# Long convolution and gated projection on one core: scratch and matrix tiles three and four deep, and the last two chunks' taps moved into the next batch's third stage

## The chip, the cores and the metric

The kernel runs on one core of one Trainium2 chip. The metric is the device time of one execution in microseconds (us); the number shown for a kernel is the median of several executions. A TensorE (PE) works out matrix products into PSUM, VectorE (DVE), ScalarE (ACT) and GpSimd (POOL) work on tiles, and SyncE (SP) issues the transfers. Each engine takes its own instructions in order.

## The reference

`x` is [8, 6400, 128] (batch, time, channel) and `h` is [6400, 128]. What is computed, cut to its core:

```
y    = irfft(rfft(x, 12800) * rfft(h, 12800))[:, :6400]      # causal convolution along time, per channel
gate = sigmoid(sum over k of conv_w[k] * shift(y, 4 - k))    # 5 taps along time, per channel
out  = (gate * (y @ w_val)) @ w_out                          # two 128x128 projections
```

All is float32.

## The kernel before

The convolution is a two-step Fourier transform written as matrix products. Time is split as 6400 = 100 x 64 (`N1`, `N2`), and the kernel goes through the eight batches one after another. A batch passes four stages, and the stages of neighbouring batches overlap:

- **First stage (`Forward`)**: 16 groups of eight channels. A group is loaded (224 KB), multiplied by `r1` on PE, and copied from PSUM to the big tile `gy` by DVE (even groups) or ACT (odd groups).
- **Second stage (`Product`)**: 13 blocks `kb` of eight frequencies (the last has four). PE multiplies a block of `gy` by a matrix tile of `m2` (512 KB, `m2_sb`, `M2B` buffers, loaded again for every batch) into a pair of PSUM banks. `swap` (ACT, two instructions) writes the real and the imaginary part exchanged into a scratch tile `w_t`; `mul_u` (DVE) multiplies the PSUM pair by one half of the filter's spectrum, `mul_t` (DVE) the scratch by the other, and `add` (POOL, DVE for the last block) puts their sum back into `gy`. The spectrum comes from DRAM, two tiles of 512 KB for each block (`h_load`, buffers for two blocks).
- **Third stage (`s3_quad`)**: 16 groups, each two PSUM banks of four channels. PE multiplies `gy` by `r3`; ACT copies the first bank (A) and DVE the second (B) to the big tile `dt`. In the same group PE does one group of the first stage for the next batch, so that `gy` is filled again.
- **Fourth stage (`Chunk`)**: the 64 rows of `N2` are cut into a head of four rows (60 to 63, worked first) and 12 chunks of five rows. For a chunk PE does 20 (head: 16) small matmuls from `dt` (`s4`) into one PSUM bank `p`; ACT copies `p` to the tile `y`, writes tap 4 scaled into the gate's rows, and tap 3 scaled into a scratch `q` (`copies`); one step later DVE adds taps 0, 1 and 2 from PSUM and POOL adds `q` (`taps`). Then `project` (PE), `sigm` (ACT), `gate` (DVE), `output` (PE) and `store` (ACT copy and transfer) follow, spread over the next steps.

The fourth stage of a batch and the second stage of the next run together in 13 steps `s` (lines 550 to 579). Step `s` holds the product `s + 1`, the `s4` and the `copies` of chunk `s`, the products' DVE work for block `s`, the `taps` of chunk `s - 1`, and `project`, `sigm` and `gate` of chunk `s - 2`, `output` of `s - 3` and `store` of `s - 4`. Step 0 has two products. Chunk 0 is the head. What is left of the last chunks (`finish`, in five pieces, `trail`) runs with the next batch's third stage: one piece before it and one behind each of its first groups. The head is finished last, since its gate rows take taps of the last chunk.

The order on each engine is the program's (`keep_in_program_order`, line 88, through which every instruction passes: so every row of the profile has L88). Semaphores between the engines, and which of the buffers of a PSUM pool a tile gets, are set by the framework when it compiles. PSUM has two pairs of banks for products and first-stage groups (`pair`, `ps2`), and four single banks (`single`, `ps1`) which third-stage banks, `p`, `project` and `output` share.

The gate's rows and `y` of the chunks below row `LATE` lie in columns of `dt` that `s4` has read already; those from `LATE` on have tiles of their own (`gl`, `yl`), because the next third stage writes `dt` while they are still worked on.

The very first part of the program works out the filter's spectrum (`Spectrum`) together with the products of batch 0, with no fourth stage beside it. In the last batch there is no next batch and so no product.

The lines that the change touches most:

```
M2B = 3
LATE = 30
w_t = [cp.tile([128, KB * C], F32, name=f"w_{i}") for i in range(2)]
self.t = kdt(w_t[kb % 2], kb)
```

Of the kernel before, what the change touches and what calls it, by code (L numbers as in the profile page):

```python
# [9 lines left out]
F32 = mybir.dt.float32  # L10
# [5 lines left out]
C = 128  # L16
N1 = 100
# [3 lines left out]
KB = 8  # L21
# [6 lines left out]
CH = 5  # L28
HEAD = (60, 4)
CHUNKS = [HEAD] + [(a, CH) for a in range(0, 60, CH)]  # L30
NCH = len(CHUNKS)
OUT_ORDER = CHUNKS[1:] + [HEAD]
LATE = 30
LATER = 7
M2B = 3
HB = 4
XB = 4

# [62 lines left out]
def longconv_moe(ctx: ExitStack, tc: tile.TileContext, x, h, r1, m2, r3, m4, w64, out):  # L101
# [4 lines left out]
    cp = ctx.enter_context(tc.tile_pool(name="cp", bufs=1))  # L106
# [12 lines left out]
    w_sb = cp.tile([C, NW], F32, name="w_sb")  # L119
    wc_sb = w_sb[:, 2 * C :]  # L120
    gl = cp.tile([128, N2 - LATE, N1], F32, name="gl")
    yl = {a: cp.tile([128, CH, N1], F32, name=f"yl_{a}") for a, _ in CHUNKS if a >= LATE}
    m2_sb = [cp.tile([128, KB, C], F32, name=f"m2_{i}") for i in range(M2B)]
    h_sb = [cp.tile([128, KB * C], F32, name=f"h_{i}") for i in range(HB)]
    x_sb = [cp.tile([PX, XG, N2], F32, name=f"x_{i}") for i in range(XB)]
    w_t = [cp.tile([128, KB * C], F32, name=f"w_{i}") for i in range(2)]
    p_t = [cp.tile([128, CH, N1], F32, name=f"p_{i}") for i in range(2)]
    hd = dp.tile([NKB, 2, 2 * N2, KB * C], F32, name="hd")

# [60 lines left out]
    act = nc.scalar.copy  # L190
# [9 lines left out]
    class Forward:  # L200


        def __init__(self, src, dst):
            self.src, self.dst, self.n, self.i = src, dst, 0, 0
# [31 lines left out]
    def count(kb):  # L236
        return min(KB, N1 - kb * KB)

    def m2_load(kb):
        if kb < NKB:  # L240
            n = count(kb)
            nc.sync.dma_start(m2_sb[kb % M2B][:, :n], m2[:, kb * KB : kb * KB + n])

    def h_load(kb):
        if kb < NKB:
            n = count(kb) * C
            for r in range(2):
                nc.sync.dma_start(h_sb[(2 * kb + r) % HB][:, :n], hd[kb, r, :, :n])
# [6 lines left out]
    def kdt(t, kb):  # L255
        n = count(kb)
        return t[:, : n * C].rearrange("p (d k t) -> p d k t", k=n, t=2)

    def s2_mm(src, kb):
        pt = pair()  # L260
        n = count(kb)
        for k in range(n):
            nc.tensor.matmul(
                pt[:, k // 4, (k % 4) * C : (k % 4 + 1) * C],
                lhsT=m2_sb[kb % M2B][:, k, :],
                rhs=src[:, :, kb * KB + k],
                start=True,
                stop=True,
            )
        if n <= 4:  # L270
            return pt[:, 0, : n * C].rearrange("p (k d t) -> p d k t", t=2, d=C // 2)
        return pt.rearrange("p b (k d t) -> p d (b k) t", t=2, d=C // 2)
# [24 lines left out]
    class Product:  # L297
        def __init__(self, kb, h=None):
            self.kb, self.v = kb, s2_mm(gy, kb)
            self.t = kdt(w_t[kb % 2], kb)  # L300
            self.u = gy[:, :, kb * KB : kb * KB + count(kb)]
            self.h = [kdt(i, kb) for i in h or [h_sb[(2 * kb + r) % HB] for r in range(2)]]

# [14 lines left out]
    def s3_quad(d0):  # L318
        pt = single()
        for q in range(4):  # L320
            d = d0 + q
            nc.tensor.matmul(
                pt[:N1, q * 2 * N2 : (q + 1) * 2 * N2],
                lhsT=gy[:, d // 2, :, d % 2],
                rhs=r3_sb,
                start=True,
                stop=True,
            )
        o = dv[:N1, :, :, d0 : d0 + 4].rearrange("p n c d -> p (n c) d")
        return lambda e: e(o, pt[:N1].rearrange("p (d m) -> p m d", d=4))  # L330
# [6 lines left out]
    def cells(x, n):  # L337

        out, i = [], 0
        while i < n:  # L340
            y = x + i
            end = 4 if y < 4 else LATE if y < LATE else N2
            k = min(n - i, end - y)
            s = (y - 4) % N2
            out.append((i, gl[:, y - LATE : y - LATE + k] if y >= LATE else dv[:, s : s + k, 1, :N1]))
            i += k
        return out

    class Chunk:


        def __init__(self, b, ch):
            self.b, self.ch = b, ch
            a, n = ch
            self.y = yl[a][:, :n] if a >= LATE else dv[:, a : a + n, 0, :N1]

        def s4(self):
# [22 lines left out]
        def copies(self):  # L380
            a, n = self.ch
            if a == HEAD[0]:
                for i, o in cells(0, n):
                    nc.gpsimd.memset(o[:, :, :1], 0.0)
                    self.first(4, o[:, :, 1:], self.p[:, i : i + n, : N1 - 1])
                act(self.y, self.p)
                for i, o in cells(a, n):
                    self.first(0, o, self.p)
                return
            k = min(n, HEAD[0] - a - 4)  # L390
            for i, o in cells(a + 4, k):
                self.first(4, o, self.p[:, i : i + o.shape[1]])
            act(self.y, self.p)
            self.q = p_t[a // CH % 2]
            self.first(3, self.q, self.p)

        def taps(self):
            a, n = self.ch
            if a == HEAD[0]:
                for j in range(1, 4):  # L400
                    for i, o in cells(a + j, n - j):
                        self.more(j, o, self.p[:, : n - j])
                    for i, o in cells(0, j):
                        self.more(j, o[:, :, 1:], self.p[:, n - j :, : N1 - 1])
                return
            k = HEAD[0] - a - 4
            if k < n:
                for i, o in cells(HEAD[0], n - k):
                    self.more(4, o, self.p[:, k:])
            for j in range(3):  # L410
                for i, o in cells(a + j, n):
                    self.more(j, o, self.p[:, i : i + o.shape[1]])
            for i, o in cells(a + 3, n):
                nc.gpsimd.tensor_tensor(out=o, in0=o, in1=self.q[:, i : i + o.shape[1]], op=ADD)

# [32 lines left out]
    for f in (fh, fx):  # L448
# [8 lines left out]
        if f is fh:  # L457
            next(wgen)
    for kb in range(M2B):
        m2_load(kb)  # L460
    nc.sync.dma_start(r3_sb, r3)
    sp, pr = {0: Spectrum(0)}, {}
    for kb in range(-1, NKB + 1):
        if 0 <= kb < NKB:
            pr[kb] = Product(kb, sp[kb].h)
            m2_load(kb + M2B)
        if kb + 2 < NKB:
# [16 lines left out]
    class Gates:  # L484


        def __init__(self, b):
            self.cs = [Chunk(b, ch) for ch in CHUNKS]

        def at(self, s, last):  # L490

# [20 lines left out]
    trail = []  # L512
# [3 lines left out]
    for b in range(B):  # L516
        nxt = b + 1 < B


        if trail:  # L520
            trail.pop(0)()
        if nxt:
            for kb in range(M2B):
                m2_load(kb)
            for kb in range(2):
                h_load(kb)
        for g in range(NG):
            e = [s3_quad(8 * g), s3_quad(8 * g + 4)]
            f = fx.group() if nxt else []
            e[0](act)  # L530
            e[1](dve)
            for i in f:
                i(act if g % 2 else dve)
            if trail:
                trail.pop(0)()
            if b == 0:
                m4_load(4 * g, 4 * g + 4)
                if LATER + g < NKB:
                    h_double(LATER + g)
                next(wgen, None)  # L540
                next(wgen, None)
        for _ in wgen:
            pass
        if b + 2 < B:
            fx = Forward(x[b + 2], gy)


        gs = Gates(b)
        ps = {}
        for s in range(NCH):  # L550
            if s == 0:
                gs.cs[0].s4()
                if nxt:
                    ps[0] = Product(0)
                    m2_load(M2B)
                    ps[0].swap()
            if nxt and s + 1 < NKB:
                ps[s + 1] = Product(s + 1)
                m2_load(s + 1 + M2B)
            gs.each("project", s - 2)  # L560
            if s:
                gs.cs[s].s4()
            gs.each("output", s - 3)
            gs.each("store", s - 4)
            if s + 1 in ps:
                ps[s + 1].swap()
            gs.each("sigm", s - 2)
            gs.cs[s].copies()
            if nxt:
                ps[s].mul_u()  # L570
            if s:
                gs.cs[s - 1].taps()
            if nxt:
                ps[s].mul_t()
                ps.pop(s).add()
                h_load(s + 2)
            gs.each("gate", s - 2)
            if s == 10 and b + 2 < B:
                fx.load(XB)
        trail = [lambda s=s, gs=gs: gs.finish(s) for s in range(NCH, NCH + 5)]  # L580
    for t in trail:
        t()

# [43 lines left out]
```

## Time and profile before

| | us |
|---|---|
| median of three runs (lowest, highest) | 1144.38 (1143.68, 1144.84) |
| the profiled execution, its own time | 1145.32 |
| its span, first to last instruction | 1143.5 |
| first part, up to the third stage of batch 0 | 119.6 |
| one batch in the middle, from the head's `s4` to the next head's | 132.7 |
| of it fourth stage / third stage | 77.4 / 55.3 |
| fourth stage of the last batch, to the end | 58.9 |

Rows of groups give an operation with its output and inputs by the program's tile names (`pt` is any PSUM tile, `m` and `m_sb` the matrices, `w` the scratch, `p` the tap scratch `q`), its shape, how often it ran and its mean duration in ns. Rows of the timeline give the start in us, the duration from the first to the last of the merged instructions, the engine, the operation, the count, and in brackets how long the engine stood idle before it and what ended that. A float32 matmul of the program is two instructions in the trace. Rows of windows give for each stretch the busy time of PE, PE's weight loads, DVE, ACT and POOL, the granted PE clock, the share of the DMA engines' time and GB/s.

### The profile page before, as it was taken

Reading aid. Unit: us, or ns where it says so; the run is one execution under the profiler, and the core shown is the slowest. Engines: PE = TensorE matmul, PEld = TensorE weight load, DVE = VectorE, ACT = ScalarE, POOL = GpSimd, SP = SyncE. Lnnn points to the kernel's source line nnn. Section 1 sums busy time; section 2 is a strip of 40 time slices with the busy share of each in tenths; the row PEclk is TensorE's granted clock in tenths of the full one; section 3 lists DMA queues with packets and bytes.
Section 4 is the critical chain, followed back from the end, with each engine's and each line's share of the span. In section 5 each row is a group of like instructions: output and inputs, shape, how many; then the busy total and the mean of one; then the engine's idle time right before and its main releaser. Section 6 shows DMA issues by size and latency. Waiting matters only on the chain.

```text
span 1143.5 us, 19606 instructions
## 1 busy us (share of the span) xinstructions
PE 1063.3 (93%) x7480; PEld 946.2 (83%) x7480; DVE 835.2 (73%) x1176; ACT 725.4 (63%) x1188; POOL 410.9 (36%) x220
## 2 busy tenths in 40 slices
PE   8987899999999899999999999999999999999998
PEld 8977898769988699777987699886997789876975
DVE  5799776975589755896569855887568956698375
ACT  5787347764478546774568655775567744786365
POOL 0044004750067301770047500773018700475022
PEclk9999899989999999999999999999999999999999
DMA  5696947974199634986279741997349862793012
GB/s 148 193 326 196 333 129 257 286 210 150 44 310 279 238 90 137 297 240 213 57 243 297 221 150 55 307 265 237 89 142 296 235 214 56 251 290 111 26 28 89
DMA packets 105163, 221.15 MB, mean 193 GB/s; under 512 B 40170, under 2 KB 49358, under 8 KB 104910
## 3 DMA queue, kind: packets, MB, share of 16 engines
q1 hardware_dynamic: 105070, 219.89, 60.6%
q8 instruction: 60, 0.98, 0.4%
q14 instruction: 33, 0.27, 0.1%
HBM read 183.42 MB, written 39.32 MB: 195 GB/s over the span
## 4 chain that ended last, share of the span: by engine, by line
PE 54%; ACT 18%; POOL 12%; DVE 9%; issue 4%; DMA 3%; POOLq 0%; DVEq 0%; SPq 0%; ACTq 0%
PE pt L88 54%; POOL gy L88 7%; ACT w L88 7%; DVE dt L88 4%; POOL dt L88 3%; ACT dt L88 3%; DVE gl L88 3%; DMA m<-m 2%; ACT yl L88 2%; ACT p L88 2%; ACT gl L88 2%; DVE gy L88 1%; ACT gy L88 1%; DVE w L88 1%; POOL gl L88 1%
## 5 line engine op out<-in xcount | busy, mean ns | idle before, releaser
L88 PEld LDWEIGHTS pt<-m_sb,dt 100*128 100x128 f32 x2048 | 242.7, 193 | 71.9 <-ACT dt L88 29.6
L88 POOL TENSOR_TENSOR gy<-gy,w 128x1024 f32<-128x1024 f32 x96 | 228.0, 2375 | 148.7 <-DVE w L88 141.1
L88 PE MATMUL pt<-m_sb,dt 100*128 100x100 f32 x2048 | 247.9, 277 | 24.9 <-ACT dt L88 14.5
L88 PEld LDWEIGHTS pt<-r_sb,gy 128*100 128x100 f32 x2048 | 240.3, 172 | 30.9 <-issue 20.6
L88 PE MATMUL pt<-r_sb,gy 128*100 128x128 f32 x2048 | 248.0, 274 | 15.2 <-DVE gy L88 8.9
L88 ACT COPY dt<-pt 100x512 f32<-100x512 f32 (+3 forms) x264 | 153.8, 582 | 160.5 <-PE pt L88 159.2
L88 PEld LDWEIGHTS pt<-gy,m 128*128 128x128 f32 x1600 | 196.7, 190 | 33.1 <-DVE gy L88 12.2
L88 PE MATMUL pt<-r_sb,x 100*128 100x200 f32 x1152 | 217.1, 336 | 4.5 <-DMA x<-hl 4.2
L88 PE MATMUL pt<-gy,m 128*128 128x128 f32 x1600 | 204.7, 280 | 10.8 <-DVE gy L88 10.8
L88 DVE COPY dt<-pt 100x512 f32<-100x512 f32 (+2 forms) x168 | 116.7, 695 | 123.4 <-PE pt L88 120.9
L88 PEld LDWEIGHTS pt<-r_sb,x 100*128 100x128 f32 x1152 | 194.0, 193 | 4.7 <-issue 4.7
L88 ACT COPY gy<-pt 64x400 f32<-64x400 f32 x256 | 124.4, 486 | 100.7 <-PE pt L88 98.5
L88 DVE COPY gy<-pt 64x400 f32<-64x400 f32 x256 | 146.5, 572 | 42.8 <-PE pt L88 40.3
L88 ACT ACTIVATE w<-pt 64x1024 f32<-64x1024 f32 (+1 forms) x104 | 102.7, 988 | 103.7 <-POOL gy L88 84.1
L88 POOL MEMSET dt<- 128x4 f32 x8 | 0.8, 106 | 419.8 <-PE pt L88 419.8
L88 DVE TENSOR_TENSOR gy<-pt,h 128x1024 f32<-128x1024 f32 (+1 forms) x100 | 117.5, 1174 | 46.2 <-ACT w L88 45.9
L88 DVE SCALAR_TENSOR_TENSOR gl<-pt,w_sb,gl 128x500 f32<-128x500 f32 (+3 forms) x192 | 126.3, 661 | 15.8 <-POOL gl L88 4.9
L88 POOL TENSOR_TENSOR gl<-gl,p 128x500 f32<-128x500 f32 (+1 forms) x56 | 99.2, 1772 | 84.0 <-DVE gl L88 81.6
L88 DVE SCALAR_TENSOR_TENSOR dt<-pt,w_sb,dt 128x500 f32<-128x500 f32 (+3 forms) x192 | 115.1, 617 | 12.6 <-POOL dt L88 5.2
L88 DVE TENSOR_TENSOR w<-w,h 128x1024 f32<-128x1024 f32 (+1 forms) x100 | 122.3, 1223 | 0.0
L88 POOL TENSOR_TENSOR dt<-dt,p 128x500 f32<-128x500 f32 (+3 forms) x56 | 85.7, 1531 | 73.3 <-DVE dt L88 61.5
L88 ACT COPY w<-pt 64x1024 f32<-64x1024 f32 (+1 forms) x104 | 101.0, 971 | 2.4
(31 smaller groups left out, 741.6 us busy)
## 6 DMA issues: line engine op xcount, KB each, us to landing
h<-hd SPq DMA_DIRECT2D x168, 512.0 KB, 5.7
m<-m SPq DMA_DIRECT2D x96, 512.0 KB, 5.4
x<-xl SPq DMA_DIRECT2D x128, 224.0 KB, 2.8
out<-dt SPq DMA_DIRECT2D x48, 250.0 KB, 5.2
out<-yl SPq DMA_DIRECT2D x48, 250.0 KB, 3.0
hd<-h SPq DMA_DIRECT2D x10, 512.0 KB, 4.9
x<-hl SPq DMA_DIRECT2D x16, 224.0 KB, 2.6
h<-hd SPq DMA_DIRECT2D x14, 256.0 KB, 4.5
```

What stands on the lines that cost most here:

```text
L88: return self._tc.keep_in_program_order(call(*args, **kwargs))
```

## The change

Four constants and tiles: `LATE` goes from 30 to 35 (chunk 30 moves into `dt`), `M2B` from 3 to 4, the scratch tiles `w_t` from 2 to 3 (`WB`), and the head's `y` tile shrinks to four rows. In step 0 the head's `copies` (ACT) stand ahead of the first product, and its `taps` (DVE) stand behind `swap(0)` and ahead of the second product; both stood behind `swap(1)` or later. In step 1 the chunk's `s4` stands ahead of product 2 instead of behind it. For the chunks at rows 50 and 55 (numbers 11 and 12; `DEFER`), in all batches but the last, `copies` writes only `y`; their taps read `y` from SBUF, tap 3 is done by DVE instead of ACT and POOL, and all of that, tap 4 included, is done in the trail. The trail has eight pieces instead of five.

```diff
-LATE = 30
+LATE = 35
+DEFER = 50
-M2B = 3
+M2B = 4
+WB = 3
-    yl = {a: cp.tile([128, CH, N1], F32, name=f"yl_{a}") for a, _ in CHUNKS if a >= LATE}
+    yl = {a: cp.tile([128, n, N1], F32, name=f"yl_{a}") for a, n in CHUNKS if a >= LATE}
-    w_t = [cp.tile([128, KB * C], F32, name=f"w_{i}") for i in range(2)]
+    w_t = [cp.tile([128, KB * C], F32, name=f"w_{i}") for i in range(WB)]
-            self.t = kdt(w_t[kb % 2], kb)
+            self.t = kdt(w_t[kb % WB], kb)
...
+            self.late = defer and DEFER <= a < HEAD[0]
...
-            k = min(n, HEAD[0] - a - 4)
-            for i, o in cells(a + 4, k):
-                self.first(4, o, self.p[:, i : i + o.shape[1]])
+            if self.late:
+                act(self.y, self.p)
+                self.p = self.y
+                return
+            self.init()
             act(self.y, self.p)
             self.q = p_t[a // CH % 2]
             self.first(3, self.q, self.p)
 
+        def init(self):
+            a, n = self.ch
+            for i, o in cells(a + 4, min(n, HEAD[0] - a - 4)):
+                self.first(4, o, self.p[:, i : i + o.shape[1]])
+
         def taps(self):
             a, n = self.ch
+            if self.late:
+                self.init()
...
-            for j in range(3):
+            for j in range(4 if self.late else 3):
                 for i, o in cells(a + j, n):
                     self.more(j, o, self.p[:, i : i + o.shape[1]])
+            if self.late:
+                return
...
+        def trail(self):
+
+            h, i, j, k = (self.cs[i] for i in (0, NCH - 3, NCH - 2, NCH - 1))
+            before = self.cs[NCH - 4]
+            return [
+                lambda c=c: [f() for f in c]
+                for c in (
+                    (j.project, i.output, before.store),
+                    (j.taps, i.store),
+                    (j.sigm, j.gate),
+                    (k.project, j.output, k.taps),
+                    (j.store, k.sigm, k.gate),
+                    (h.project, k.output, h.sigm, h.gate),
+                    (h.output, k.store),
+                    (h.store,),
+                )
+            ]
...
             if s == 0:
                 gs.cs[0].s4()
+                gs.cs[0].copies()
                 if nxt:
                     ps[0] = Product(0)
                     m2_load(M2B)
                     ps[0].swap()
+                gs.cs[0].taps()
+            if s == 1:
+                gs.cs[s].s4()
             if nxt and s + 1 < NKB:
                 ps[s + 1] = Product(s + 1)
                 m2_load(s + 1 + M2B)
             gs.each("project", s - 2)
-            if s:
+            if s > 1:
                 gs.cs[s].s4()
...
-            gs.cs[s].copies()
+            if s:
+                gs.cs[s].copies()
             if nxt:
                 ps[s].mul_u()
-            if s:
+            if s > 1 and not gs.cs[s - 1].late:
                 gs.cs[s - 1].taps()
...
-        trail = [lambda s=s, gs=gs: gs.finish(s) for s in range(NCH, NCH + 5)]
+        trail = gs.trail() if nxt else [lambda s=s: gs.finish(s) for s in range(NCH, NCH + 5)]
```

More of the change, by code (lines that the diff above doesn't have):

```diff
@@ L349, in longconv_moe, with __init__ @@
     class Chunk:
-        def __init__(self, b, ch):
+        def __init__(self, b, ch, defer):
             self.b, self.ch = b, ch
             a, n = ch
+            self.late = defer and DEFER <= a < HEAD[0]
             self.y = yl[a][:, :n] if a >= LATE else dv[:, a : a + n, 0, :N1]
@@ L484, in longconv_moe, with __init__ @@
     class Gates:
-        def __init__(self, b):
-            self.cs = [Chunk(b, ch) for ch in CHUNKS]
+        def __init__(self, b, defer):
+            self.cs = [Chunk(b, ch, defer) for ch in CHUNKS]
+        def trail(self):
[14 more added lines that the diff above has]
+            ]
         def at(self, s, last):
@@ L545, in longconv_moe @@
             fx = Forward(x[b + 2], gy)
-        gs = Gates(b)
+        gs = Gates(b, nxt)
         ps = {}
```

## The prediction

> **What bounds the kernel now.** The page first: PE is busy 93% of the span of 1143.5 us.
>
> ```profile
> PE 1063.3 (93%) x7480; PEld 946.2 (83%) x7480; DVE 835.2 (73%) x1176; ACT 725.4 (63%) x1188; POOL 410.9 (36%) x220
> ```
>
> So I look for the places where PE stands, and how dense its work is where it doesn't. The timeline of batch 1 gives both; its batch runs from 307.93 to 440.63 by the chain of waits (132.7 us), and its parts stand below. First the dense part of the fourth stage and of the third:
>
> ```profile
> 309.87 3.96 PE L88 MATMUL pt<-gy,m 128*128 128x128 f32 x32
> ...
> 354.94 2.00 PE L88 MATMUL pt<-gy,m 128*128 128x128 f32 x16
> 356.79 1.00 PE L88 MATMUL pt<-dt,w_sb 128*128 128x500 f32 x2
> 357.62 2.37 PE L88 MATMUL pt<-m_sb,dt 100*128 100x100 f32 x20
> 359.83 1.03 PE L88 MATMUL pt<-dt,w_sb 128*128 128x500 f32 x2
> 360.69 2.01 PE L88 MATMUL pt<-gy,m 128*128 128x128 f32 x16
> ...
> 427.92 1.91 PE L88 MATMUL pt<-r_sb,gy 128*100 128x128 f32 x16
> 431.02 1.91 PE L88 MATMUL pt<-r_sb,gy 128*100 128x128 f32 x16
> ```
>
> From start to start a product costs 1.85 us, a project 0.83, an `s4` 2.21, an output 0.86: 5.75 for a full step, with no gap. A third-stage group costs 3.10. The fourth stage from 307.93 to 385.37 (the first third-stage matmul below) is 77.4 us. Its PE work alone: 12.5 products 23.1, the head's `s4` 1.94 (307.93 to 309.87), twelve `s4` 26.5, eleven projects 9.1, ten outputs 8.6, sum 69.3. So PE stands 8.1 us there. The third stage has 16 x 3.10 and about 3.9 of trail matmuls, 53.5, against 55.3 measured: 1.8 more. These are the stands:
>
> ```profile
> 307.93 4.07 PE pt L88 x32
> 440.63 4.07 PE pt L88 x32
> ...
> 314.10 1.23 DVE L88 TENSOR_TENSOR gy<-pt,h 128x1024 f32<-128x1024 f32 x1 [6.31 <-ACT w L88]
> 315.38 2.12 PE L88 MATMUL pt<-gy,m 128*128 128x128 f32 x16 [1.54 <-DVE gy L88]
> 329.81 1.02 ACT L88 ACTIVATE w<-pt 64x1024 f32<-64x1024 f32 x1 [2.56 <-POOL gy L88]
> 334.43 2.09 PE L88 MATMUL pt<-gy,m 128*128 128x128 f32 x16
> 338.65 0.58 ACT L88 COPY dt<-pt 128x500 f32<-128x500 f32 x1
> 339.29 2.48 PE L88 MATMUL pt<-m_sb,dt 100*128 100x100 f32 x20 [1.49 <-ACT dt L88]
> 349.18 2.02 PE L88 MATMUL pt<-gy,m 128*128 128x128 f32 x16
> ...
> 379.17 2.48 PE L88 MATMUL pt<-m_sb,dt 100*128 100x100 f32 x20 [1.05 <-ACT yl L88]
> 383.20 0.67 DVE L88 TENSOR_TENSOR gl<-pt,gl 128x500 f32<-128x500 f32 x1
> 383.59 1.10 PE L88 MATMUL pt<-yl,w_sb 128*128 128x500 f32 x2 [1.08 <-ACT yl L88]
> 383.79 2.81 DVE L88 SCALAR_TENSOR_TENSOR gl<-pt,w_sb,gl 128x400 f32<-128x400 f32 x4
> 385.37 1.04 PE L88 MATMUL pt<-r_sb,gy 128*100 128x128 f32 x8
> 387.08 1.12 PE L88 MATMUL pt<-r_sb,gy 128*100 128x128 f32 x8 [0.67 <-ACT dt L88]
> ```
>
> Three groups. **Start**: product 2 (315.38) needs the PSUM pair of product 0, which `mul_u(0)` frees at 315.33; PE was done with product 1 at 309.87 + 2 x 1.85 = 313.57, so 1.8 us are lost. **Middle**: `swap(4)` (329.81) waits 2.56 us for POOL's `add(2)`, because both use the same scratch tile; ACT stays that late, its store copy of chunk 1 (338.65) frees a PSUM bank late, and `s4(5)` starts 0.06 us after it ended. From product 6 (334.43) to product 8 (349.18) are 14.75 us, dense would be two steps, 11.5: 3.2 lost. Product 9 (354.94) follows after 5.76, and so on: from here the old kernel is dense. **End**: `s4(12)` (379.17) and project 11 (383.59) wait for ACT's store copies, 1.2 and 1.3 us against the dense spacing, while DVE has three taps of chunk 11 and four of chunk 12 (383.79) to do.
>
> **The change, part by part.**
>
> *Step 0 and 1 reordered.* The head's copies and taps ran here:
>
> ```profile
> 316.15 0.59 ACT L88 ACTIVATE dt<-pt,w_sb 128x396 f32<-128x396 f32 x1
> 317.01 0.61 ACT L88 ACTIVATE gl<-pt,w_sb 128x400 f32<-128x400 f32 x1
> 317.65 0.53 DVE L88 SCALAR_TENSOR_TENSOR gl<-pt,w_sb,gl 128x300 f32<-128x300 f32 x1
> 319.22 0.52 DVE L88 SCALAR_TENSOR_TENSOR dt<-pt,w_sb,dt 128x297 f32<-128x297 f32 x1
> 315.35 1.46 SPq L88 DMA_DIRECT2D h<-hd  x2
> h<-hd SPq DMA_DIRECT2D x20, 512.0 KB, 5.7
> ```
>
> Copies 1.47 us (316.15 to 317.62), taps 2.09 (317.65 to 319.74). Moved, the copies run from 310.1 (head's `s4` out) to 311.6, inside ACT's wait for product 0, which ended at 312.0 anyway; the taps from 311.6 to 313.7, inside DVE's wait of 6.31 us that ends at 314.10. So both are covered, with 0.4 us to spare; without that cover 3.6 us would stand ahead of `mul_u(0)`. `s4(1)` now fills PE from 313.6 to 315.8, and product 2 starts then, its pair free since 315.33. What is late next is `mul_u(2)`: its spectrum is issued at 315.35 and lands 5.7 us later, at 321.05, so product 4 starts at about 322.3 instead of 323.63. The start is worth 1.3 us: the 1.8, less 0.5 of new wait.
>
> *Third scratch tile.* `swap(4)` then needs `add(1)`, a step older, instead of `add(2)`, and its 2.56 us go. Chunk 1's store copy, which ended at 339.23, ends by that and by the 1.3 us of the start at 335.4; PE, dense from product 6 on, wants the bank at 334.43 + 1.85 + 0.83 - 1.3 = 335.8. The middle is worth 3.2 us if the framework hands out the banks as before; nothing if another bank's release takes that place. I take 3.2: the wait follows ACT's delay to 0.06 us, and that delay has one cause. DVE comes closest behind: in the window of 356 to 360 below it is busy 3.93 of 4 us.
>
> *The taps of chunks 11 and 12 out of steps 12 and the first trail piece.* They take three and four DVE instructions (3 x 0.74 = 2.2 by the row below, and 2.81 above), two ACT scratches and two POOL adds out of the end, so ACT's store copies come in time and the stands of 1.2 and 1.3 go: 2.5 us. DVE goes `mul_u(12)`, `mul_t(12)`, `add(12)`, `gate(10)` without taps between. `gate(10)` (383.20) ended at 383.87, 0.6 ahead of output 10 (385.37 - 0.86 = 384.5); it comes 2.2 earlier against PE's 2.5, which leaves 0.3. Bounds: if it is late, up to its 0.67 us is lost; above, no more than the 2.5.
>
> *The same taps in the third stage.* No row shows such a tap from SBUF. The nearest:
>
> ```profile
> L88 DVE SCALAR_TENSOR_TENSOR gl<-gl 128x261 f32<-128x261 f32 x1 | 0.4, 432 | 0.0
> L88 DVE SCALAR_TENSOR_TENSOR gl<-pt,w_sb,gl 128x500 f32<-128x500 f32 x144 | 106.0, 736 | 11.0 <-POOL gl L88 4.9 <-issue 2.6
> L88 DVE SCALAR_TENSOR_TENSOR gl<-pt,w_sb,gl 128x100 f32<-128x100 f32 x16 | 5.0, 313 | 0.0
> L88 DVE COPY gy<-pt 64x400 f32<-64x400 f32 x256 | 146.5, 572 | 42.8 <-PE pt L88 40.3
> 390.00:440.00 50.00, 49.73 (x367) 47.73 (x367) 29.06 (x49) 24.16 (x47) 0.00 (x0) 1.00 0.36 118
> ```
>
> With the PSUM rows' slope, (736 - 313)/400 = 1.06 ns an element, 500 elements from SBUF come to 0.69 us; 0.74 is the other bound; I take 0.70. Train one is four of them, 2.8 us; train two five, 3.4. The window shows DVE 58% busy there and POOL idle. By hand from the third stage's start: DVE has the first-stage copies of group 0 (4 x 0.57) from 3.3 to 5.6, so train one runs from 5.6 to 8.4; the B copy, sigmoid and gate behind it, some 0.6 each, end near 10, and PE asks for that gate behind three groups and project 12, at 3 x 3.10 + 0.83 = 10.1: nothing lost. Train two stands behind group 2's gate, B copy and first-stage copies, from 13 to 16.4, and holds the B copy of group 3 and ACT's sigmoid. PE comes to group 4's second bank at 4 x 3.10 + 1.7 + 0.9 = 15.0, when project 12, output 11 and two copies not made hold all four; the first comes free near 16.8, by the store copy of chunk 11. That is 1.8 us, and I add 0.4 for small ones: 2.2. The 1.8 us lost there now, which come from the same banks while chunk 12's taps hold one (387.08), go. So the third stage costs 0.4 more; bounds: 1.8 us less, and 8.6 more with both trains and what follows them uncovered (worked out below).
>
> *Nothing, and why.* The fourth matrix tile: in steps 1 to 12 no PE row waits for a matrix. In the first part PE does, but DVE is full there (43.25 of 44 us), so what the matrices free, DVE keeps; without that cover it would be worth up to the 8.9 us that PE waits:
>
> ```profile
> 63.00:107.00 44.00, 36.98 (x290) 35.63 (x291) 43.25 (x37) 34.98 (x35) 21.38 (x9) 0.96 0.87 292
> L88 PE MATMUL pt<-dt,m 128*128 128x128 f32 x200 | 26.4, 285 | 9.4 <-DMA m<-m 8.9 <-ACT h L88 0.3
> out<-dt SPq DMA_DIRECT2D x48, 250.0 KB, 5.2
> 240.00:256.00 16.00, 13.58 (x61) 8.54 (x60) 11.70 (x16) 8.40 (x16) 7.22 (x4) 0.79 0.62 201
> 356.00:360.00 4.00, 4.00 (x32) 3.54 (x31) 3.93 (x5) 3.47 (x6) 2.34 (x2) 1.00 1.00 305
> ```
>
> `LATE`: chunk 30's store now reads `dt`, and the third stage's first copy into `dt` must wait for it. It is issued in step 11; behind it lie step 12 without its product (4 us), project 11, output 10 and the first bank (1.7 + 1.0), and the landing takes 5.2: covered by some 1.5 us, and what it is late would be the price. SP's issue order ahead of it doesn't change. SP: its stores move behind the loads of `x` of groups 0 to 6, four groups (12 us) ahead of use. The last batch has no product, so no scratch wait; 0.
>
> *The clock.* In the window at batch 0's end the granted clock is 0.79: 0.21 x 16 = 3.4 us of clock lost, at a place where PE stood about 1 us at a time. With those stands gone I count half, 1.7. The Trainium skill ("TensorE: Matmul & The Clock Gate", Part 1: The HAM clock gate) has the clock halved after an idle window of about 3.4 us. By that rule the new kernel's gaps are too short to lose any clock, and the whole 3.4 comes back; but the trace loses it with gaps near 1 us, so the trace decides and I keep half.
>
> **Sum.** Per batch 1.3 + 3.2 + 2.5 - 0.4 = 6.6, for the seven batches with a product: 46.2. Clock 1.7. The last third stage, without the first-stage group, has 1.9 us of PE work per group instead of 3.10 and hides a train less well: minus 1. Together 46.9 off the profiled execution's 1145.3 (its span and 1.8 around it): 1098.4. That run lies 0.9 above the median of 1144.4, so 1097.5, or 1098.
>
> **The rivals.**
>
> *Stage four stays where transfers or banks put it* (0.20). For it: the DMA share is 1.00 at 305 GB/s in the last window above, and a denser PE asks for the same bytes sooner; the bank's new owner is the framework's choice. Against it: loads are asked for two steps (11.5 us) ahead and land in 5.7. If the middle stays as it is, 7 x 3.2 = 22 less: 1120.
>
> *The fourth matrix tile pays in the first part* (0.08): 8.9 more: 1089. Against it, DVE's full window.
>
> *Slower: the tap trains hold the third stage* (0.07). Place: groups 1 to 4, with four single banks, of which project 11 and output 10 hold two. If neither train is covered, PE loses each train and the sigmoid, the gate and the B copy behind it, 0.7 each: 4.9 and 5.5, 10.4 in all, less the 1.8 it loses now: 8.6 more, against 7.0 won in the fourth stage: 1.6 x 7 = 11 slower: 1155. It decides once the third stage is over 55.3 + 7.0 = 62 us long. For it: ACT's sigmoid waits behind each train and holds the next A copy. Against it: PE is 10 us away when train one ends.
>
> *Nothing comes of it* (0.03): third stage and fourth cancel: 1144.
>
> **How the numbers follow.** Forecast 0.62. Its own range: no new spectrum wait, a third stage as long as now and the clock all back, 7 x 0.9 + 1.7 = 8 more and with the first part's 8.9 partly, 1086; 1.5 us more in each third stage and a third of the middle lost, 7 x 2.5, 1115. The range 1083 to 1130 takes in the first two rivals and leaves out some 0.17. A run of this kernel tells about 0.2%, 2.3 us, from no change: faster 0.90, same 0.03, slower 0.07.
>
> **What would show it.** Right: product 2 starts behind `s4(1)` with no wait; `swap(4)` no longer ends on POOL; `s4(5)`, `s4(6)`, `s4(12)` and project 11 without waits; fourth stage near 70.5 us, third near 55.7, with a wait of one to two us near group 4; the first part unchanged at 119.6. Wrong: a third stage above 58, DVE waiting for the spectrum in later steps, or the dense step longer than 5.75.

## The result, and the profile after

The changed kernel takes 1104.78 us (median of four runs, 1102.62 to 1106.83), against 1144.03 for the kernel before on the same chip (1142.93 to 1144.84): a ratio of 0.9652, 95% interval 0.9638 to 0.9666. The profiled execution took 1102.62, 42.7 less than the one profiled before. The forecast was 1098, the range 1083 to 1130.

The engines' shares on the page of the changed kernel:

```profile
PE 1050.3 (95%) x7480; PEld 941.0 (85%) x7480; DVE 860.8 (78%) x1190; ACT 724.2 (66%) x1174; POOL 390.8 (36%) x206
PE 74%; ACT 13%; DVE 9%; issue 3%; DMA 1%; POOL 0%; POOLq 0%; SPq 0%; DVEq 0%; ACTq 0%
h<-hd SPq DMA_DIRECT2D x168, 512.0 KB, 6.6
```

The second row is the chain that ended last: POOL is gone from it (12% before). The third is a new number to keep in mind: the spectrum now takes 6.6 us from issue to landing, 5.7 before.

By the first matmul of each stage, the middle of the program compares so (us; a step is named by its product or `s4`, counted from the head's `s4` of one batch in the middle):

| | product 4 | 6 | 8 | 12 | third stage starts | third stage lasts | batch |
|---|---|---|---|---|---|---|---|
| before | 15.69 | 26.49 | 41.24 | 64.29 | 77.42 | 55.27 | 132.7 |
| after | 13.89 | 24.65 | 36.66 | 59.70 | 71.05 | 56.20 | 127.25 |

The fourth stage is 6.4 us shorter, the third 0.9 longer. The timeline of PE in batch 2 of the changed kernel, from the head's `s4` at 425.22 to the next head's, cut to the stages' joints and to every wait that it shows:

```profile
425.22 2.00 PE L90 MATMUL pt<-m_sb,dt 100*128 100x100 f32 x16
427.15 3.96 PE L90 MATMUL pt<-gy,m 128*128 128x128 f32 x32
430.96 2.37 PE L90 MATMUL pt<-m_sb,dt 100*128 100x100 f32 x20
433.17 3.90 PE L90 MATMUL pt<-gy,m 128*128 128x128 f32 x32
...
439.11 2.03 PE L90 MATMUL pt<-gy,m 128*128 128x128 f32 x16
...
449.84 2.04 PE L90 MATMUL pt<-gy,m 128*128 128x128 f32 x16
452.10 1.10 PE L90 MATMUL pt<-dt,w_sb 128*128 128x500 f32 x2 [0.22 <-ACT dt L90]
...
484.92 1.08 PE L90 MATMUL pt<-gy,m 128*128 128x128 f32 x8
486.49 1.10 PE L90 MATMUL pt<-yl,w_sb 128*128 128x500 f32 x2 [0.49 <-ACT dt L90]
...
496.26 1.91 PE L90 MATMUL pt<-r_sb,gy 128*100 128x128 f32 x16
...
504.21 1.52 PE L90 MATMUL pt<-r_sb,x 100*128 100x200 f32 x8
505.82 1.10 PE L90 MATMUL pt<-yl,w_sb 128*128 128x500 f32 x2
...
510.70 1.04 PE L90 MATMUL pt<-r_sb,gy 128*100 128x128 f32 x8
513.52 1.12 PE L90 MATMUL pt<-r_sb,gy 128*100 128x128 f32 x8 [1.78 <-ACT yl L90]
514.48 1.52 PE L90 MATMUL pt<-r_sb,x 100*128 100x200 f32 x8
...
550.81 1.52 PE L90 MATMUL pt<-r_sb,x 100*128 100x200 f32 x8
552.46 2.00 PE L90 MATMUL pt<-m_sb,dt 100*128 100x100 f32 x16
```

The 1.54 ahead of product 2, the 1.49 ahead of `s4(5)` and the 1.05 and 1.08 at the end are gone. In their place stand 0.22 ahead of project 3 and 0.49 ahead of project 9, both for a store copy of ACT, and 1.78 in group 4 of the third stage for the store copy of chunk 11.

### The profile page after: what moved, and what is told of

The parts are those of the page before. It is cut to its first block, busy times and chain, and to the rows that moved or that the text cites. A ratio compares the mean times of both kernels' runs of the same rounds, so it can differ in the third digit from the quotient of the medians.

```text
span 1100.8 us, 19538 instructions
## 1 busy us (share of the span) xinstructions
PE 1050.3 (95%) x7480; PEld 941.0 (85%) x7480; DVE 860.8 (78%) x1190; ACT 724.2 (66%) x1174; POOL 390.8 (36%) x206
## 4 chain that ended last, share of the span: by engine, by line
PE 74%; ACT 13%; DVE 9%; issue 3%; DMA 1%; POOL 0%; POOLq 0%; SPq 0%; DVEq 0%; ACTq 0%
PE pt L90 74%; ACT w L90 5%; ACT dt L90 4%; DVE gy L90 2%; DVE gl L90 2%; ACT p L90 2%; DVE dt L90 2%; DVE w L90 1%; ACT gy L90 1%; DVE h L90 1%; ACT yl L90 1%; DMA h<-hd 1%; ACT gl L90 1%; POOL dt L90 0%; DMA x<-hl 0%
## 5 line engine op out<-in xcount | busy, mean ns | idle before, releaser
L90 ACT COPY dt<-pt 100x512 f32<-100x512 f32 (+3 forms) x280 | 163.1, 583 | 152.4 <-PE pt L90 148.9
L90 PE MATMUL pt<-m_sb,dt 100*128 100x100 f32 x2048 | 243.7, 274 | 3.5 <-DVE dt L90 2.6
L90 PE MATMUL pt<-gy,m 128*128 128x128 f32 x1600 | 201.4, 279 | 1.7 <-DVE dt L90 1.6
L90 DVE TENSOR_TENSOR w<-w,h 128x1024 f32<-128x1024 f32 (+1 forms) x100 | 147.4, 1474 | 0.0
L90 DVE SCALAR_TENSOR_TENSOR dt<-pt,w_sb,dt 128x500 f32<-128x500 f32 (+7 forms) x216 | 132.7, 630 | 12.0 <-POOL dt L90 6.1
L90 POOL TENSOR_TENSOR dt<-dt,p 128x500 f32<-128x500 f32 (+1 forms) x64 | 101.4, 1585 | 58.6 <-DVE dt L90 32.9
L90 PE MATMUL pt<-dt,w_sb 128*128 128x500 f32 (+2 forms) x240 | 114.0, 564 | 2.8 <-ACT dt L90 2.7
L90 DVE SCALAR_TENSOR_TENSOR gl<-pt,w_sb,gl 128x500 f32<-128x500 f32 (+3 forms) x119 | 74.0, 623 | 39.2 <-ACT gl L90 30.1
```

Source lines behind the costliest of these rows:

```text
L90: return self._tc.keep_in_program_order(call(*args, **kwargs))
```

## The experiments

The theory: three gains (start, middle, end), each of a cause of its own, less a small price in the third stage. The rival reading: the three wait for one another, so that a part alone brings nothing or several times its share. Each part was added alone to the kernel before, and each was taken back alone from the changed kernel. Each ratio is against runs of the kernel before taken beside that kernel, so it is not the quotient of two times of this table. A batch in the middle, from the traces (us):

| kernel | time | ratio (interval) | fourth stage | third stage |
|---|---|---|---|---|
| before | 1144.03 | 1 | 77.42 | 55.27 |
| scratch alone | 1125.8 | 0.9834 (0.9812 to 0.9855) | 75.25 | 55.27 |
| order alone | 1144.06 | 1.0000 (0.9989 to 1.0012) | 77.4 to 77.6 | 55.27 |
| deferral alone | 1140.6 | 0.9974 (0.9954 to 0.9993) | 75.4 to 75.9 | 56.21 |
| all but scratch | 1143.27 | 0.9985 (0.9973 to 0.9997) | 75.8, or 77.5 | 56.20 |
| all but order | 1112.93 | 0.9720 (0.9695 to 0.9746) | 72.35 | 56.20 |
| all but deferral | 1118.06 | 0.9776 (0.9762 to 0.9791) | 73.91 | 55.27 |
| all | 1104.78 | 0.9652 (0.9638 to 0.9666) | 71.05 | 56.20 |

Where a fourth stage has two values, the longer one belongs to batches in which PE runs at half clock for 3.4 or 6.8 us behind a stand of 1.5 us ahead of `s4(5)`.

**Scratch alone**, in the kernel before:

```diff
-    w_t = [cp.tile([128, KB * C], F32, name=f"w_{i}") for i in range(2)]
-            self.t = kdt(w_t[kb % 2], kb)
+    w_t = [cp.tile([128, KB * C], F32, name=f"w_{i}") for i in range(3)]
+            self.t = kdt(w_t[kb % 3], kb)
```

> The kernel before with a third scratch tile and nothing else. Theory: the middle's 2.7 us go in seven batches, the start's 1.8 and the end's 2.5 stay: 19 us, about 1125. Rival (another PSUM bank or the spectrum takes the place of the wait): above 1138.

Measured 1125.8. Product 8 starts at 37.98 instead of 41.24: the middle is worth 3.26, and no `swap` waits for POOL. But from product 12 to the third stage it now takes 14.2 us where it took 13.1, so the stage gains only 2.2. The timeline of PE, batch 1 of this kernel, its only waits at the end:

```profile
364.46 1.10 PE L88 MATMUL pt<-yl,w_sb 128*128 128x500 f32 x2 [0.49 <-ACT yl L88]
370.06 1.11 PE L88 MATMUL pt<-yl,w_sb 128*128 128x500 f32 x2 [1.42 <-ACT yl L88]
375.32 1.10 PE L88 MATMUL pt<-yl,w_sb 128*128 128x500 f32 x2 [1.08 <-ACT yl L88]
```

PE comes to the end sooner, ACT and DVE have as much to do there as before, and PE stands at three projects; in the kernel before it stood twice (1.05 and 1.08). The time came out as expected, but not by the sum: 7 x 2.2 is 15, not 19. The rest is luck of the clock: the kernel before has half-clock periods in batches 0 and 4, this one has none between the first part and the last batch.

**All but scratch**, in the changed kernel:

```diff
-WB = 3
+WB = 2
```

> The changed kernel with two scratch tiles instead of three. Theory (the third scratch is needed by the middle and by the reordered start alike): the fourth stage loses the middle's 2.7 us and, because swap 2 again waits for POOL's add 0, the start's 1.8 too: 4.5 x 7 = 31 us above the changed kernel's 1105, about 1136. Rival (the parts add up, scratch is worth only the middle): 2.7 x 7 = 19, about 1124.

Measured 1143.27, hardly faster than before. Without the third scratch the other two parts are worth 1.6 us of the fourth stage, and the third stage takes 0.9 of that back. ACT's and PE's timelines in batch 2, and a row of windows over the middle:

```profile
447.90 1.02 ACT L90 ACTIVATE w<-pt 64x1024 f32<-64x1024 f32 x1 [2.91 <-POOL gy L90]
458.66 1.02 ACT L90 ACTIVATE w<-pt 64x1024 f32<-64x1024 f32 x1 [3.14 <-POOL gy L90]
```

```profile
468.15 3.61 PE L90 MATMUL pt<-m_sb,dt 100*128 100x100 f32 x20 [1.50 <-ACT dt L90]
```

```profile
466.00:474.00 8.00, 6.50 (x28) 4.86 (x27) 6.78 (x9) 6.02 (x11) 7.35 (x4) 0.70 0.85 271
```

`swap(2)` and `swap(4)` wait for POOL's `add` again, and `s4(5)` for ACT, as before the change. The last row holds what the expectation left out: the granted clock is 0.70 there, since in four of the seven batches PE runs at half clock for 6.8 us behind that stand. Those batches have a fourth stage of 77.5, the others 75.8: 1.7 each. With 7 x 4.75 for the stages (75.8 against 71.05) that makes 40 us, 38.5 measured.

**Order alone**, in the kernel before (steps 0 and 1 as in the diff of the change, nothing else):

> The kernel before with steps 0 and 1 in the new order and nothing else. Theory (with two scratch tiles swap 2 waits for POOL's add 0 as before, so what PE wins at product 2 is lost by product 4 to 6): at most 0.5 us a batch, 1140 to 1144. Rival (the parts add up): 1.8 x 7 = 12.7 us, about 1131.

Measured 1144.06, no change. PE's and ACT's timelines, batch 1, with the head's `s4` at 306.29:

```profile
306.29 2.00 PE L88 MATMUL pt<-m_sb,dt 100*128 100x100 f32 x16
...
314.24 3.89 PE L88 MATMUL pt<-gy,m 128*128 128x128 f32 x32
...
320.76 2.12 PE L88 MATMUL pt<-gy,m 128*128 128x128 f32 x16 [0.42 <-DVE gy L88]
...
337.65 3.01 PE L88 MATMUL pt<-m_sb,dt 100*128 100x100 f32 x20 [1.49 <-ACT dt L88]
```

```profile
317.40 1.02 ACT L88 ACTIVATE w<-pt 64x1024 f32<-64x1024 f32 x1 [2.91 <-POOL gy L88]
```

Products 2 and 3 (314.24) follow without a gap, as they should. But `swap(2)` starts 11.1 us behind the head's `s4` (317.40 - 306.29), and so it did in the kernel before, whose row (ACT's timeline, batch 1, head at 307.93) is

```profile
319.03 1.02 ACT L88 ACTIVATE w<-pt 64x1024 f32<-64x1024 f32 x1 [1.42 <-POOL gy L88]
```

In both it waits for `add(0)` on POOL, whose chain of `swap(0)`, `mul_u(0)` and `mul_t(0)` the new order doesn't move. So product 4 waits for `mul_u(2)`. Of the 1.8 us of the start 1.2 are left there (14.47 behind the head's `s4` instead of 15.69) and none at product 6 (26.50 and 26.49).

**All but order**, in the changed kernel (the head's `copies` and `taps` and the first `s4` back in their old places):

> The changed kernel with steps 0 and 1 in the old order. Both theories: product 2 waits again for the PSUM pair, 1.8 us in each of seven batches: 12.7 us, about 1117. If the start is hidden anyway by something later in the stage: 1105 to 1108.

Measured 1112.93, 8.1 slower than with it. The fourth stage is 1.30 longer in six of the seven batches, and only 0.2 in batch 0 (72.54 against 72.37): 8.0 in all. With three scratches the start is worth what was forecast, and with two it is worth nothing.

**Deferral alone**, in the kernel before (`DEFER`, `late`, the longer `trail`; two scratches, `LATE` 30, old order):

> The kernel before with the taps of the last two chunks moved into the third stage and the trail of eight pieces, nothing else. Theory: the end wins 1.8 to 2.5 us, the third stage loses 0.9: 0.9 to 1.6 x 7 = 6 to 11 faster, 1133 to 1138. Rival (with two scratch tiles ACT is too late for the end to win anything): 1144 to 1150.

Measured 1140.6, between theory and no change. In the batches at full clock the fourth stage gains 2.0 (75.4), as the theory had it; in the four with a half-clock period it gains 1.5. The third loses 0.94. At 1.5 that is 7 x 0.56 = 3.9, at 2.0 it would be 7.4.

**All but deferral**, in the changed kernel:

```diff
-        gs = Gates(b, nxt)
-        trail = gs.trail() if nxt else [lambda s=s: gs.finish(s) for s in range(NCH, NCH + 5)]
+        gs = Gates(b, False)
+        trail = [lambda s=s, gs=gs: gs.finish(s) for s in range(NCH, NCH + 5)]
```

> The changed kernel with the taps of the last two chunks back in steps 12 and the first trail piece, and the old trail of five pieces. Theory: the fourth stage gets 1.8 to 2.5 us longer, the third 0.9 shorter: 0.9 to 1.6 x 7 = 6 to 11 slower, 1111 to 1116. Rival (the trains in the third stage cost as much as the end gains): within 3 us of 1105.

Measured 1118.06. Here the fourth stage is 2.86 longer, with waits of 0.49, 1.41 and 1.08 at the same three projects as with the scratch alone, and the third 0.93 shorter: 7 x 1.9 = 13.5. Deferral is worth 2.9 once the scratch brings PE to the end early, and 2.0 in the kernel before at full clock.

**Nothing from the matrix tile and from `LATE`**: the changed kernel with three matrix tiles, and with three and `LATE` back at 30.

```diff
-LATE = 35
-M2B = 4
+LATE = 30
+M2B = 3
```

> The changed kernel with three matrix tiles instead of four. Theory (DVE fills the first part, the matrices were only the last of several things PE waited for): the first part is 117.9 to 119.6 us long, the whole 1105 to 1107. Rival (the matrix waits of 8.9 us were on the path): about 1113.

> The changed kernel with chunk 30 back in its own tiles (30 instead of 35) and three matrix tiles. Theory (both tile changes are neutral: the store of chunk 30 lands ahead of the next third stage, and the matrices are covered by DVE): 71.05 and 56.2 us for the two stages, 1104 to 1108. Rival (the transfer from dt costs the end something): the fourth stage 0.5 us shorter, about 1102.

Measured 1106.86 (0.9680, interval 0.9666 to 0.9695) and 1107.36 (0.9677, 0.9657 to 0.9696), stages of 71.05 and 56.20, 71.03 and 56.20. Both intervals touch or overlap the changed kernel's. With three matrix tiles and `LATE` at 35, two batches have a third stage of 57.9 at half clock, the changed kernel one. The first part takes 118.8 to 120.3 us in five of the six kernels with three matrix tiles (122.9 with the deferral alone) and 117.9 to 119.9 in those with four, so the fourth tile is worth about one microsecond there at most. The group of the first part's products and the window over it, in the changed kernel:

```profile
L90 PE MATMUL pt<-dt,m 128*128 128x128 f32 x200 | 25.9, 281 | 8.6 <-DVE h L90 5.8 <-DVE dt L90 2.7
62.00:106.00 44.00, 35.53 (x290) 33.88 (x289) 43.25 (x37) 37.46 (x39) 21.30 (x10) 1.00 0.85 277
```

PE waits 8.6 us there, as long as before (9.4), but for DVE now and no longer for the matrices: DVE's 43.25 of 44 us were the limit all along.

**Chunk 11's store copy first.** The 1.78 us in group 4 should go if ACT's store copy of chunk 11 is not queued behind the second tap train:

```diff
-                    (k.project, j.output, k.taps),
-                    (j.store, k.sigm, k.gate),
+                    (k.project, j.output, j.store, k.taps),
+                    (k.sigm, k.gate),
```

> The changed kernel with the store of chunk 11 one trail piece earlier, ahead of the second train. Theory (PE's wait of 1.78 us in group 4 of the third stage is for the PSUM bank that this store copy frees): that wait goes, 1.8 x 7 = 12 us faster than the changed kernel, about 1093. Rival (the train itself holds PE, through the B copy, whose bank is then the one that is missing): 1100 to 1105.

Measured 1094.8 (1094.2 to 1098.89; ratio 0.9573, 0.9551 to 0.9594), about 10 us under the changed kernel. The third stage falls to 54.28, below that of the kernel before. PE's timeline in group 4 of batch 2:

```profile
507.63 1.91 PE L90 MATMUL pt<-r_sb,gy 128*100 128x128 f32 x16
509.38 1.52 PE L90 MATMUL pt<-r_sb,x 100*128 100x200 f32 x8
```

Both banks of the group now run without a break (x16 in one row, where the changed kernel has x8, a stand, x8). The gain of 1.92 a batch doesn't all arrive: six such batches and batch 4's clock give 13.2, the profiled execution is 8.4 faster. In the last batch the third stage is 1.1 longer (35.7), with a new stand of 1.15 us ahead of project 12, and the fourth stage is 2.6 longer, with a half-clock period of 6.8 us that the changed kernel's profile doesn't have.

**The other store copies earlier too.** The waits of 0.22 and 0.49 in the fourth stage are for store copies. Here each step's copy goes ahead of ACT's tap-3 scratch, one step sooner than before:

```diff
-            gs.each("store", s - 4)
...
-                gs.cs[s].copies()
+                gs.cs[s].copies(lambda: gs.each("store", s - 3))
```

> The kernel with the early store of chunk 11, and in the fourth stage every store copy one place earlier on ACT, between the copy of y and the tap-3 scratch. Theory (project 3 and project 9 wait for the PSUM bank that the store copy of chunk 1 and of chunk 7 frees, 0.4 to 0.5 us and the refill behind it each): the fourth stage of a middle batch falls from 71.05 to about 70.0, 7 us in all, 1088. Rival (the scratch, now later, holds the taps and with them the bank of p, or DVE is the next to be late): 71 or more, 1094 to 1100.

Measured 1103.0, 8 us slower than without it. Both waits did go (product 8 starts 36.21 behind the head's `s4`, `s4(12)` 65.18 against 66.20), but the fourth stage takes 71.6 to 72.8. DVE's and SP's timelines, batch 2:

```profile
492.36 0.69 DVE L90 TENSOR_TENSOR gy<-pt,h 128x512 f32<-128x512 f32 x1 [1.72 <-DMA h<-hd]
```

```profile
485.04 0.55 SPq L90 DMA_DIRECT2D out<-dt  x1
485.68 1.15 SPq L90 DMA_DIRECT2D h<-hd  x2
```

`mul_u(12)` waits for the last block of the spectrum, and SP issued its loads at 485.68, right behind a store that had itself waited for ACT's copy. The group of `mul_u` has it for the whole program:

```profile
L90 DVE TENSOR_TENSOR gy<-pt,h 128x1024 f32<-128x1024 f32 (+1 forms) x100 | 117.7, 1177 | 29.6 <-DMA h<-hd 23.0 <-ACT w L90 3.1 <-ACT dt L90 1.5
```

23.0 us of waits for the spectrum, where the changed kernel has 3.8. That left open whether SP's order or the transfers' bandwidth (DMA share 0.84 to 0.94 from 486 to 496 us) is the cause. So the next kernel turns SP's order alone: a step's store transfer is issued behind its spectrum loads, while ACT's copies stay.

```diff
             act(self.y, self.o)
-            i, k = _out_range(self.ch)
+            if send:
+                self.send()
...
                 h_load(s + 2)
+            if gs.at(s - 3, False):
+                gs.cs[s - 3].send()
```

> The kernel with every store copy inside its step, with one thing moved: the transfer of a store inside a step is issued by SP behind the two spectrum loads of that step instead of ahead of them; the copy on ACT stays where it was. In that kernel SP issued the store of chunk 8 at 485.04 us, when ACT's copy was there, and the loads of the last spectrum block right behind it at 485.68, though the buffer of its first half was free at about 481.5; and VectorE then stood 1.72 us for that spectrum. Theory (the store's own wait held the loads behind it in SP's queue): the first half is asked for some 4 us sooner, VectorE's wait for it at the end is gone, and the fourth stage falls from about 72 to between 70 and 70.6 us, the third stays at 54.3; the time is 1103 - 7 x 1.8 = 1090, about 5 us under the kernel that only moved chunk 11's copy. Rival (the transfers are limited by the bandwidth there, at a DMA share of 0.84 to 0.92): the spectrum lands as late as before, the wait stays over 1 us, and the time is 1100 or more.

Measured 1092.56 (1092.09 to 1095.01; ratio 0.9552, 0.9536 to 0.9568), 10.4 faster than with the stores first. The same group, then SP's and DVE's timelines, batch 2:

```profile
L90 DVE TENSOR_TENSOR gy<-pt,h 128x1024 f32<-128x1024 f32 (+1 forms) x100 | 117.4, 1174 | 8.1 <-DMA h<-hd 4.1
```

```profile
480.90 0.32 SPq L90 DMA_DIRECT2D h<-hd  x1
482.49 0.55 SPq L90 DMA_DIRECT2D out<-dt  x1
```

```profile
487.05 0.68 DVE L90 TENSOR_TENSOR gy<-pt,h 128x512 f32<-128x512 f32 x1
487.65 2.88 DVE L90 TENSOR_TENSOR w<-w,h 128x512 f32<-128x512 f32 x1
```

The load is asked for ahead of the store, `mul_u(12)` runs without a wait, and 4.1 us of such waits are left of 23.0, with the same bytes to move: the order in SP's queue was the cause, not the bandwidth. The theory's 70 to 70.6 us for the fourth stage was a little low (70.6 to 71.4), and against the kernel that only moved chunk 11's copy the gain of 5 us didn't come: the two intervals overlap.

The control turns SP's order in that simpler kernel, the copies left where they were:

> The changed kernel with chunk 11's store copy moved ahead of the second tap train, and the same turn of SP's order (a step's store transfer behind its spectrum loads) with the store copies where they were. There the stores come at the start of a step and hold the loads little: VectorE's waits for the spectrum are 3.4 us in all. Theory: at most these 3 us, so between 1092 and 1095, no difference that can be told from 1094.8; the fourth stage 71.0 or just below. Rival (SP's order matters in every step): the fourth stage falls by half a microsecond or more, and the time is under 1091.

Measured 1093.88 (0.9558, 0.9544 to 0.9573), fourth stage 71.05: no difference that can be told from 1094.8. Where stores come at the start of a step, their place ahead of the loads costs nothing that shows. Three kernels thus stand at 1093 to 1095, all about 4.4% faster than before, and the two lines of the trail are what they have in common.

## Why the prediction was right, and where its steps were not

- **Start, 1.3: the size was right, the place of the loss was not.** 1.30 and 1.34 were measured (all against all but order; all but deferral against scratch alone). The working had product 4 late by 0.5 for the spectrum. It isn't: it starts at 13.89, dense, 1.8 earlier than before. Some 0.4 goes later, at project 3 (449.84 to 452.10 instead of 1.85), which waits for the store copy of chunk 1. The price stands only with the third scratch, which the working treated as a matter of its own, and not in batch 0, where the order is worth 0.2.
- **Middle, 3.2: right.** 3.26 at product 8 in the kernel with the scratch alone. In the changed kernel product 8 comes 4.58 earlier (41.24 to 36.66): start and middle together, 4.5 forecast. No `swap` of a middle batch waits for POOL.
- **End, 2.5: the term that was sized too high, 1.8 net** (13.13 to 11.35 from product 12). The working took the end's waits of the kernel before as they stood. Two things had changed by then: PE arrives over 4 us sooner, which by itself lengthens the end by 1.1 (14.2, with the scratch alone and with all but deferral), and deferral takes 2.86 off that. What is left stands ahead of project 9: from the half product at 484.92 to 486.49 are 1.57 us, dense 0.93. It waits for the store copy of chunk 7, which ACT does behind the three instructions of chunk 10's `copies`, from the step before, and ends at 486.44 (ACT's timeline, batch 2 of the changed kernel):

```profile
485.86 0.58 ACT L90 COPY dt<-pt 128x500 f32<-128x500 f32 x1
```

- **Third stage, 0.4 more: sized too low, 0.94.** Three terms make it. The new wait was where the working put it, in group 4, for chunk 11's store copy: from 510.70 to 514.48 are 3.78 us instead of 1.75, 2.03 lost (forecast 1.8). The small ones are 0.36 at project 12 (forecast 0.4): it comes 1.61 behind the first-stage group of 504.21 instead of 1.36, since its gate stands behind the first tap train, and takes 0.1 longer to follow up. But the waits that went were worth 1.45, not 1.8 (in the trace before group 0 takes 0.93 and group 2 0.52 more than 3.10): 0.3 of what stood over the dense sum lies at the joint to the next head's `s4` (550.81 to 552.46 are 1.65 instead of 1.36), before the change as after it. 2.03 + 0.36 - 1.45 = 0.94. The size of a tap from SBUF was off as well, without harm. DVE's timeline, and the group of these taps:

```profile
501.98 3.06 DVE L90 SCALAR_TENSOR_TENSOR gl<-yl,w_sb,gl 128x500 f32<-128x500 f32 x4
509.33 3.61 DVE L90 SCALAR_TENSOR_TENSOR gl<-yl,w_sb,gl 128x400 f32<-128x400 f32 x5
```

```profile
L90 DVE SCALAR_TENSOR_TENSOR gl<-yl,w_sb,gl 128x500 f32<-128x500 f32 x56 | 41.4, 739 | 1.7
```

A tap from SBUF takes 739 ns, as one from PSUM does (736): of the two bounds the upper, and I took 0.70. Both trains begin where the working had them (5.7 and 13.1 us into the stage) and are 0.2 to 0.3 longer.
- **Nothing for `LATE` and the fourth matrix tile: right**, the cover too (DVE's full window).
- **Last third stage, minus 1:** 0.78, from 33.78 to 34.56.
- **The clock, 1.7:** right in sign, with luck in size. The fourth stage wins 2.3 beyond a middle batch's share in batch 0 and 1.8 in batch 4, where the profile before had its periods of half clock (the working had only the first); but the new stand in group 4 met one of its own and lost 1.7 again.
- **The sum.** A middle batch gains 5.43 instead of 6.6: seven times, 38.0 instead of 46.2. The other 4.7 of the profiled 42.7 are the first part (1.7 us less, within what it varies by), the clock and the ends. The working had 0.7 for these (1.7 of clock, less 1), so they made up 4 of the 8.2 us that the stages fell short by, and that was luck. None of the rivals came: banks didn't keep the middle, the third stage is nowhere near 62 us, and the matrix tile pays at most about a microsecond.

What the forecast lacked is the interplay: the scratch is worth 2.2 us of fourth stage alone and 4.8 with the other two, the order 0 or 1.3, deferral 2.0 or 2.9. For the stages the sum came as close as it did because it was made for all parts at once, with each wait of the timeline used once.

## What to carry to other kernels

A wait that several edits touch has no price for each of them: here a tile of 512 KB decided whether an earlier start was worth 8 us or nothing, since the slower chain (scratch, `add`, next `swap`) set the pace. Before work is put into a stage with spare time, look at what its bank or tile releases are queued behind: one store copy moved ahead of a tap train brought another 10 us. And an engine's early copy can turn into a late load, if the transfer it releases stands ahead of that load in the issuing queue.

## What the runs showed of the hardware that was not expected

**Half clock behind short stands.** In the changed kernel's batch 4, PE stood 1.8 us in group 4, and the group behind it ran at half clock (PE's timeline, then the window):

```profile
768.04 1.12 PE L90 MATMUL pt<-r_sb,gy 128*100 128x128 f32 x8 [1.78 <-ACT yl L90]
769.00 2.36 PE L90 MATMUL pt<-r_sb,x 100*128 100x200 f32 x8
```

```profile
768.00:774.00 6.00, 5.96 (x25) 4.74 (x26) 4.07 (x8) 1.42 (x3) 0.00 (x0) 0.72 0.26 82
```

The first-stage group takes 2.36 us where the other batches have 1.52, the clock in the window is 0.72, and that batch's third stage is 1.69 longer than its neighbours'. Between the first part and the last batch, the clock's records of these kernels show half clock in periods of 3.4 or 6.8 us, behind stands of one to about two microseconds, but not in every batch that has such a stand: one of seven here behind the 1.78 in group 4; behind the 1.5 ahead of `s4(5)` one of seven in the kernel before, three with the order alone, and four with the deferral alone and without the third scratch; none with the scratch alone, though every batch stands 1.4 and 1.1 us at its end. The Trainium skill ("TensorE: Matmul & The Clock Gate", Part 1: The HAM clock gate) has the clock halved after an idle window of about 3.4 us. The length of the periods agrees with such a window; that a whole window has to be idle doesn't, since no stand ahead of these periods is that long. What picks the batch stays open: no run varied it.

**Two inputs from SBUF beside POOL.** The 128x512 `mul_t(12)` takes three times as long as before the change. The groups of `mul_t(12)`, the kernel before and then the changed one:

```profile
L88 DVE TENSOR_TENSOR w<-w,h 128x512 f32<-128x512 f32 x8 | 7.3, 911 | 0.0
```

```profile
L90 DVE TENSOR_TENSOR w<-w,h 128x512 f32<-128x512 f32 x8 | 22.8, 2846 | 0.0
```

Without taps in between it now starts within 0.02 us of POOL's `add(11)`; DVE's and POOL's timelines, batch 2 of the changed kernel:

```profile
490.58 2.88 DVE L90 TENSOR_TENSOR w<-w,h 128x512 f32<-128x512 f32 x1
```

```profile
490.56 2.37 POOL L90 TENSOR_TENSOR gy<-gy,w 128x1024 f32<-128x1024 f32 x1
```

It ends at 493.46, half a microsecond behind POOL (492.93). The Trainium skill ("SBUF — State Buffer", SBUF: two separate sides) says that a DVE instruction with two SBUF inputs and a POOL instruction that reads SBUF share a port pair, and that the later one waits for the whole of the other; the rows agree. The kernel before pays in the next DVE instruction, `add(12)`, which has two SBUF inputs as well and meets POOL's add of a tap scratch (DVE's and POOL's timelines, batch 1):

```profile
381.66 1.62 DVE L88 TENSOR_TENSOR gy<-gy,w 128x512 f32<-128x512 f32 x1
```

```profile
381.17 1.56 POOL L88 TENSOR_TENSOR gl<-gl,p 128x500 f32<-128x500 f32 x1 [0.74 <-DVE gl L88]
```

In the changed kernel `add(12)` takes 0.69 us. So of the 1.9 us that `mul_t(12)` grew by, about 0.8 come back there (1.50 us on average before). It cost nothing that shows in the changed kernel, where output 10 has no wait. In the kernel with the spectrum's loads first it did: there PE stood 0.30 us for the gate behind it, row

```profile
491.91 1.10 PE L90 MATMUL pt<-gl,w_sb 128*128 128x500 f32 x2 [0.30 <-DVE gl L90]
```
